# Loading q and k with 8 tokens per partition, four heads at a time, in an attention and mixer kernel

## The chip, the cores and the metric

The kernel runs on one core of a Trainium2 chip. Times are device microseconds (us) of one execution, and medians of several executions. "Fast" and "slow" are the states that each run is sorted into; comparisons use fast runs alone. A run's profile gives the span of the instructions (about 2 us less than the time) and the mean clock that TensorE was granted, as a share of full speed.

## The reference

Two stages for a batch of 8. First causal attention with 8 heads, 576 tokens and a head size of 64, with a bias from a running sum of `s`; then an MLP mixer on the result, over tokens (576 to 256 and back) and over channels (512 to 1536 and back), each with a residual.

```python
# cut to what matters
cum = np.cumsum(np.maximum(s, 0.0), axis=-1)
scores = q @ k.T / 8 + minimum(-(cum[i] - cum[j]), 0), causal
attn = softmax(scores);  x = attn @ v                       # per head
h = np.maximum(x.T @ w_tok1, 0.0) @ w_tok2;  u = x + h.T
out = u + np.maximum(u @ w_ch1, 0.0) @ w_ch2
```

All inputs and the output are float32; the kernel computes in bfloat16 with float32 sums.

## The kernel before

A small planner in the kernel's own Python orders all work: every piece (`P.op`) has an engine (or several to choose from), an estimated duration, the buffers that it reads and writes, and a priority. The planner simulates the five engines and fixes the order of instructions on each. On the chip every engine then keeps to its list and waits where something is late (in after ScalarE idled 7.56 us in front of a square, with an exp behind it whose input had been there for over 6 us; the timeline is below). All loads and stores are issued by SyncE, and loads keep their order (`after=last[0]`).

q and k are loaded for a pair of heads. A partition `p` takes R = 6 consecutive tokens of a head, one row of 6 x 64 x 4 = 1536 bytes, so 96 partitions hold 576 tokens. GpSimd casts them to bfloat16 (`qkn`), TensorE transposes them, and ScalarE takes a sum of squares for a guard: if a sum or the range of `cum` is too large, a slow general program computes everything again. That guard does not change the result here.

```python
R = 6;  PR = S // R                                  # 96 partitions
r_qf = ring("qkf", 3, [PR, 2, 2, R, D], FP32)        # partition, k/q, head of pair, token, d
r_qn = ring("qkn", 3, [PR, 2, R, 2, D], BF16)
r_vf = ring("vf", 2, [128, NJ, H, D], FP32)          # v of one batch, all five chunks

def stage_qk(b, h):
    f, n = Buf(r_qf), Buf(r_qn)
    for i, src in enumerate((k, q)):
        def load(i=i, src=src):
            nc.sync.dma_start(out=f.t[:, i].rearrange("p e r d -> p e (r d)"),
                              in_=src[b, h : h + 2].rearrange("e (p r) d -> p e (r d)", r=R))
        load_op(load, [(f, i)], 192 * 0.094 / 16)
        def cast(e, i=i): ...                        # GpSimd; in batch 0 also VectorE or ScalarE
    if b < 2:
        return
    col = (b * H + h) // 2                           # one square of 1536 elements for k, q and both heads
    P.op({"ACT": (1.55, 2.0, lambda: nc.scalar.activation(out=junk[:, :], in_=n.t[...], func=AF.Square,
          accum_out=sq[:, col : col + 1]))}, reads=[(n, 0), (n, 1)], writes=[("sq", col)], prio=60)

def stage_sq(b, h): ...        # batches 0 and 1: q and k loaded once more, later, for their squares

def mk(jc=jc, n=n):            # VectorE's causal mask: two inputs from SBUF, 5 per pair, 160 in all
    nc.vector.tensor_tensor(out=E.t[:, :, d0 : d0 + n], in0=E.t[:, :, d0 : d0 + n],
                            in1=keep[...].to_broadcast([128, 2, n]), op=ALU.mult)

def mul(eng, c=c, n=n, p0=p0): # v times its weights, GpSimd from batch 1 on: 5 per batch
    eng.tensor_tensor(out=vp.t[...], in0=vf.t[p0 : p0 + n, c], in1=wT[...], op=ALU.mult)
```

Of the kernel before, what the change touches and what calls it, by code (L numbers as in the profile page):

```python
# [333 lines left out]
def kernel(  # L334
# [24 lines left out]
    AHEAD = 4  # L359
    WARM = 45.0  # L360
    TOK = 2.0
    R = 6
# [32 lines left out]
    r_qf = ring("qkf", 3, [PR, 2, 2, R, D], FP32)  # L395
# [4 lines left out]
    r_vf = ring("vf", 2, [128, NJ, H, D], FP32)  # L400
# [56 lines left out]
    one_sb = sb("one_sb", [64, S], FP32, fast)  # L457
    cum = sb("cum", [64, S], FP32)
    half = sb("half", [64, 1], FP32, fast)
# [3 lines left out]
    nc.vector.memset(one_sb[:, :], 1.0)  # L463
# [5 lines left out]
    def act(n, fn, bias=False):  # L469
# [6 lines left out]
        out=cum[:, :], data0=one_sb[:, :], data1=s_sb[:, :], initial=0.0, op0=ALU.mult, op1=ALU.add))},  # L476
# [9 lines left out]
    def w_tr():  # L486
# [13 lines left out]
    NSQ = B * H // 2  # L500
    sq = sb("sq", [PR, NSQ], FP32, fast)
    junk = sb("junk", [PR, 4 * R * D], BF16, fast)
    pre = sb("pre", [64, S], FP32, fast)
    gap = sb("gap", [64, 4], FP32, fast)
    bad = sb("bad", [128, 4 + NSQ], FP32, fast)
    ones = sb("ones", [128, 1], FP32, fast)
# [3 lines left out]
    nc.vector.memset(ones[:, :], 1.0)  # L510

    P.op({"DVE": (1.3, 1.6, lambda: nc.vector.tensor_tensor_scan(
        out=pre[:, :], data0=one_sb[:, :], data1=wn[:, 0:S], initial=0.0, op0=ALU.mult, op1=ALU.add))},
# [16 lines left out]
    def stage_v(b):  # L530
        vf, vp = Buf(r_vf), Buf(r_vp[b % 2])
        odd = b % 2
        vbuf[b] = vp
        for c in range(NJ):
            n = min(128, S - c * 128)
            p0 = 64 if odd and n < 128 else 0

            def load(c=c, n=n, p0=p0):
                nc.sync.dma_start(out=vf.t[p0 : p0 + n, c, :, :],
                                  in_=v[b, :, c * 128 : c * 128 + n, :].rearrange("h p d -> p h d"))  # L540
            load_op(load, [(vf, c)] + ([("st", "v")] if b == 1 else []), 1024 * 0.0226 / 16 * n / 128)
        for c in range(NJ):
            n = min(128, S - c * 128)
            p0 = 64 if odd and n < 128 else 0

            def mul(eng, c=c, n=n, p0=p0):
                cw = c + 1 if p0 else c
                eng.tensor_tensor(  # L548
                    out=vp.t[p0 : p0 + n, c, :, 0:D], in0=vf.t[p0 : p0 + n, c, :, :],
                    in1=wT[p0 : p0 + n, cw, b * H : b * H + H].unsqueeze(2).to_broadcast([n, H, D]), op=ALU.mult)  # L550
            alts = ({"DVE": (*c_dve(512), lambda mul=mul: mul(nc.vector))} if b == 0 else
                    {"POOL": (*c_pool(512, 0.0019), lambda mul=mul: mul(nc.gpsimd))})
            P.op(alts, reads=[(vf, c), "wT"], writes=[(vp, c)], prio=b * 10 + 5 if b else 0)

        def ones():
            nc.gpsimd.tensor_copy(out=vp.t[:, 0 : NJ - 1, :, D], in_=wT[:, 0 : NJ - 1, b * H : b * H + H])
            p0, cw = (64, NJ) if odd else (0, NJ - 1)
            nc.gpsimd.tensor_copy(out=vp.t[p0 : p0 + 64, NJ - 1, :, D], in_=wT[p0 : p0 + 64, cw, b * H : b * H + H])
        P.op({"POOL": (0.5, 0.7, ones)}, reads=["wT"], writes=[(vp, "w")], prio=b * 10 + 5)
# [3 lines left out]
    def stage_qk(b, h):  # L563
        f, n = Buf(r_qf), Buf(r_qn)
        qkn[(b, h)] = n
        for i, src in enumerate((k, q)):
            def load(i=i, src=src):
                nc.sync.dma_start(out=f.t[:, i, :, :, :].rearrange("p e r d -> p e (r d)"),
                                  in_=src[b, h : h + 2, :, :].rearrange("e (p r) d -> p e (r d)", r=R))
            load_op(load, [(f, i)], 192 * 0.094 / 16)  # L570

            def cast(e, i=i):
                o, a = n.t[:, i, :, :, :], f.t[:, i, :, :, :].rearrange("p e r d -> p r e d")
                if e == 0:
                    nc.gpsimd.tensor_copy(out=o, in_=a)  # L575
                elif e == 1:
                    nc.vector.tensor_copy(out=o, in_=a)
                else:
                    nc.scalar.copy(out=o, in_=a)
            alts = {"POOL": (*c_pool(768, 0.0010), lambda cast=cast: cast(0))}  # L580
            if b == 0:
                alts["DVE"] = (*c_dve(768), lambda cast=cast: cast(1))
                alts["ACT"] = (*c_act(768), lambda cast=cast: cast(2))
            P.op(alts, reads=[(f, i)], writes=[(n, i)], prio=b * 10 + h if b else 0)
        if b < 2:
            return
        col = (b * H + h) // 2
        P.op({"ACT": (1.55, 2.0, lambda: nc.scalar.activation(
            out=junk[:, :], in_=n.t[:, :, :, :, :].rearrange("p t r e d -> p (t r e d)"), func=AF.Square,
            accum_out=sq[:, col : col + 1]))}, reads=[(n, 0), (n, 1)], writes=[("sq", col)], prio=60)  # L590

    def stage_sq(b, h):
        f = Buf(r_qf)
        col = (b * H + h) // 2
        for i, src in enumerate((k, q)):
            def load(i=i, src=src):
                nc.sync.dma_start(out=f.t[:, i, :, :, :].rearrange("p e r d -> p e (r d)"),
                                  in_=src[b, h : h + 2, :, :].rearrange("e (p r) d -> p e (r d)", r=R))
            load_op(load, [(f, i)], 192 * 0.094 / 16)
        P.op({"ACT": (1.55, 2.0, lambda: nc.scalar.activation(  # L600
            out=junk[:, :], in_=f.t[:, :, :, :, :].rearrange("p t e r d -> p (t e r d)"), func=AF.Square,
            accum_out=sq[:, col : col + 1]))}, reads=[(f, 0), (f, 1)], writes=[("sq", col)], prio=60)
# [3 lines left out]
    def pair(b, h):  # L606
# [6 lines left out]
        for ti, dst in ((0, kT), (1, qT)):  # L613
# [7 lines left out]
            P.op({"PE": (R * 0.045, R * 0.045 + 0.3, tr)}, reads=[(nat, ti)] + pads, writes=[(pt, 0)], holds=[dst], prio=(np_, 2))  # L621
# [87 lines left out]
    def view(t):  # L709
# [7 lines left out]
             "v": view(r_vf.tiles[1]), "uT": view(r_uTb.tiles[0]), "x2": view(r_x.tiles[2]),  # L717
             "x1": view(r_x.tiles[1]), "of": r_o.tiles[3][:, :]}
# [40 lines left out]
    def load_ch2(g):  # L759
        slot, c0, n = (("v", 0, 3), ("b0", 3, 3), ("b1", 6, 3), ("x1", 9, 2), ("of", 11, 1))[g]  # L760
# [12 lines left out]
    def tok(b):  # L773
# [31 lines left out]
        for c in range(NJ):  # L805
# [14 lines left out]
            P.op(dve(512, add), reads=[(pm, 0)] + xkeys, writes=[ukey], prio=0)  # L820
# [30 lines left out]
    def chan(b, u, us, uT):  # L851
# [26 lines left out]
        for ci, c in enumerate((4, 0, 1, 2, 3) if odd else (0, 1, 2, 3)):  # L878
            pm, o = Buf(r_mx, False), Buf(r_o, False)
            for th in range(3):  # L880
                def mm(c=c, pm=pm, th=th):
                    for cc in range(th * 4, th * 4 + 4):
                        nc.tensor.matmul(out=pm.t[:, :], lhsT=g.t[:, cc, c * 128 : c * 128 + 128], rhs=wc2[:, cc, :],  # L883
                                         start=(cc == 0), stop=(cc == NCC - 1))
                P.op({"PE": (4 * c_pe(512)[0], 4 * c_pe(512)[0] + 0.3, mm)}, reads=gkeys + [("wc2", i) for i in range(5)],
                     writes=[(pm, 0)], holds=[o], prio=(rank + 2.0 + 2.0 * ci / NJ, 1))
            if odd:
                src, si = (us, 0) if c == NJ - 1 else (u, c)
            else:
                src, si = u, c  # L890
            sk = [(us, 0, 0), (us, 0, 64)] if src is us else [(u, si, 0)]

            def add(pm=pm, o=o, src=src, si=si):
                nc.vector.tensor_tensor(out=o.t[:, :], in0=pm.t[:, :], in1=src.t[:, si, :], op=ALU.add)
            P.op(dve(512, add), reads=[(pm, 0)] + sk, writes=[(o, 0)] + ([("st", "of")] if b == 0 else []), prio=0)

            def st(o=o, c=c):
                if c < NJ - 1:
                    nc.sync.dma_start(out=out[b, c * 128 : c * 128 + 128, :], in_=o.t[:, :])
                else:  # L900
                    for i in range(2):
                        nc.sync.dma_start(out=out[b - 1 + i, NQ:S, :], in_=o.t[i * 64 : i * 64 + 64, :])
            P.op({"SP": (0.6 if c < NJ - 1 else 1.2, 0, st)}, reads=[(o, 0)], prio=0, dma=128 * 0.088 / 16)

    for h in range(0, H, 2):
        stage_qk(0, h)
        if h == 4:
            stage_v(0)
    load_tok()
    for h in range(0, AHEAD, 2):  # L910
        stage_qk(1, h)
    for i in range(4):
        load_ch1(i)
    for i in range(5):
        load_ch2(i)
    for b in range(1, B):
        for h in range(0, H, 2):
            if b > 1 or h >= AHEAD:
                stage_qk(b, h)
            if h == (0 if b > 1 else 4):  # L920
                stage_v(b)
    for b in range(2):
        for h in range(0, H, 2):
            stage_sq(b, h)
    for b in range(B):
# [5 lines left out]
    P.op(dve(64, lambda: nc.vector.tensor_scalar(  # L931
        out=bad[0:PR, 4:], in0=sq[:, :], scalar1=21.0, scalar2=None, op0=ALU.is_gt)),
        reads=[("sq", i) for i in range(NSQ)] + ["bad0"], writes=["bad"], prio=50)
# [85 lines left out]
```

## Time and profile before

| | before |
|---|---|
| median time | 331.1 us (331.06 to 331.87, 3 runs) |
| span, mean granted clock | 330.5 us, 0.982 |
| TensorE, VectorE, ScalarE, GpSimd busy | 93%, 63%, 63%, 31% |
| q and k rows | 15360 packets of 1536 bytes, mean 95 ns |
| first channel matmul of batches 0 and 1 | 42.7 and 81.6 us |

The page of before: busy time by engine, the granted clock of TensorE over 40 equal slices in tenths, and the queue of all loads and stores (packets, MB, the time of its packets as a share of 16 DMA engines).

```profile
span 330.5 us, 6536 instructions
PE 308.9 (93%) x2424; PEld 178.6 (54%) x2457; DVE 207.2 (63%) x511; ACT 207.4 (63%) x367; POOL 101.1 (31%) x137
...
PEclk9699999999999999999999999999999989999998
...
q1 hardware_dynamic: 77232, 53.64, 65.7%
```

The windows view of before: start and end of the window, its length, busy us (and instructions) of PE, PEld, DVE, ACT and POOL, the granted clock, the share of the 16 DMA engines and GB/s.

```profile
0.00:30.00 30.00, 24.40 (x195) 13.27 (x199) 23.92 (x67) 17.91 (x30) 15.78 (x34) 0.89 1.03 240
30.00:60.00 30.00, 27.69 (x228) 18.97 (x232) 20.45 (x42) 21.24 (x40) 15.67 (x18) 1.00 1.07 296
60.00:90.00 30.00, 26.75 (x286) 17.03 (x288) 26.99 (x67) 22.42 (x39) 19.75 (x23) 1.00 1.11 253
90.00:150.00 60.00, 59.21 (x468) 32.95 (x472) 38.80 (x98) 41.20 (x71) 21.34 (x27) 1.00 0.61 142
150.00:270.00 120.00, 117.05 (x934) 67.93 (x944) 79.25 (x200) 81.94 (x143) 28.53 (x36) 0.99 0.63 155
```

In each of the windows up to 90 us the DMA queue is full (a share of 1.03, 1.07 and 1.11: packets overlap), and TensorE is not (busy 24.40, 27.69 and 26.75 of 30 us); after 90 us TensorE is nearly always busy (59.21 of 60 us up to 150).

Two groups of the lines view (busy us, mean ns; then the engine's idle time just before them): ScalarE's squares of a pair for one of the three buffers, and the masks on one of the three `E` tiles.

```profile
L671 DVE TENSOR_TENSOR E_84<-E_84,keep 128x256 bf16<-128x256 bf16 (+1 forms) x55 | 17.2, 343 | 11.1 <-ACT E_84 L663 10.6
...
L588 ACT ACTIVATE junk<-qkn_77 96x1536 bf16<-96x1536 bf16 x8 | 11.9, 1489 | 0.0
```

TensorE's longest wait (line waiting, what for: us in total, times, longest):

```profile
PE psc_112 L657 <- ACT E_86 L663: 2.1, 1, 2.1
```

This is a single wait, behind a square (L600) whose reload was late; nothing else in the list is over 1.2 us.

### The profile page before, as it was taken

The numbers are of one execution on the slowest core, as the hardware profiler recorded it, in microseconds if no ns is written. First come the engines' busy times: TensorE is split into PE (matmuls) and PEld (weight loads), VectorE is DVE, ScalarE is ACT, GpSimd is POOL, SyncE is SP. The second block draws the span as 40 slices with busy tenths as digits, with TensorE's granted clock in tenths as the row PEclk, the third lists the DMA queues.
The fourth block names the chain that finished last, engine by engine and source line by source line (L and its number), as shares of the span: only waits on it lengthen the run. The fifth ranks groups of instructions, "written<-read, shape, count | busy, mean of one in ns | idle before, by whom it ended". The sixth has DMA issues, their size and how long they took to land.

```text
span 330.5 us, 6536 instructions
## 1 busy us (share of the span) xinstructions
PE 308.9 (93%) x2424; PEld 178.6 (54%) x2457; DVE 207.2 (63%) x511; ACT 207.4 (63%) x367; POOL 101.1 (31%) x137
## 2 busy tenths in 40 slices
PE   6888899979899999999999999999999799999992
PEld 2455486646665555555774554556764355446640
DVE  7698963789965756576776566576786454450021
ACT  4675777388886367974885278766889457406600
POOL 5455429757518022450146011821110000000000
PEclk9699999999999999999999999999999989999998
DMA  7999999999982549636944649266459710042031
GB/s 194 212 271 350 387 228 248 244 285 225 244 179 74 127 155 223 148 84 196 196 94 119 155 158 221 76 110 219 121 138 204 217 70 0 1 129 81 3 98 69
DMA packets 77272, 54.14 MB, mean 164 GB/s; under 512 B 54320, under 2 KB 70256, under 8 KB 77232
## 3 DMA queue, kind: packets, MB, share of 16 engines
q1 hardware_dynamic: 77232, 53.64, 65.7%
q8 instruction: 21, 0.34, 0.5%
q14 instruction: 19, 0.16, 0.2%
HBM read 40.65 MB, written 9.44 MB: 152 GB/s over the span
## 4 chain that ended last, share of the span: by engine, by line
PE 75%; DVE 14%; ACT 3%; DMA 3%; issue 2%; SPq 1%; POOL 0%; ACTq 0%
PE pmx_118 L883 12%; PE pmx_119 L865 9%; PE pmx_118 L865 8%; PE pmx_117 L865 8%; PE pmx_117 L883 7%; PE pmx_119 L883 7%; PE psc_112 L657 3%; PE pav_115 L689 2%; PE psc_113 L657 2%; PE psc_114 L657 2%; PE pav_116 L689 2%; DMA qkf_73<-in_k_dram 2%; PE pmx_117 L791 2%; PE pmx_117 L812 2%; DVE E_86 L671 2%
## 5 line engine op out<-in xcount | busy, mean ns | idle before, releaser
L865 PEld LDWEIGHTS <-wc_70 128*128 128x128 bf16 x624 | 59.2, 98 | 30.7 <-issue 0.5
L883 PEld LDWEIGHTS <-gb_107 128*128 128x128 bf16 x240 | 22.8, 99 | 25.6 <-issue 1.3
L575 POOL CAST qkn_75<-qkf_72 96x768 bf16<-96x768 f32 x19 | 17.1, 923 | 43.2 <-issue 12.9
L575 POOL CAST qkn_76<-qkf_73 96x768 bf16<-96x768 f32 x22 | 18.3, 853 | 37.2 <-issue 18.2
L883 PE MATMUL pmx_118<-wc_71,gb_107 128*128 128x512 bf16 x116 | 28.9, 393 | 0.2
L883 PEld LDWEIGHTS <-ga_106 128*128 128x128 bf16 x192 | 18.0, 98 | 19.6
L575 POOL CAST qkn_77<-qkf_74 96x768 bf16<-96x768 f32 x19 | 15.7, 843 | 30.7 <-ACT gb_107 L872 10.3
L671 DVE TENSOR_TENSOR E_84<-E_84,keep 128x256 bf16<-128x256 bf16 (+1 forms) x55 | 17.2, 343 | 11.1 <-ACT E_84 L663 10.6
L865 PE MATMUL pmx_118<-uTb_105,wc_70 128*128 128x320 bf16 x128 | 22.6, 299 | 0.1
L865 PE MATMUL pmx_119<-uTb_105,wc_70 128*128 128x320 bf16 x128 | 22.6, 299 | 0.0
L865 PE MATMUL pmx_117<-uTb_105,wc_70 128*128 128x320 bf16 x128 | 22.6, 299 | 0.0
L671 DVE TENSOR_TENSOR E_85<-E_85,keep 128x256 bf16<-128x256 bf16 (+1 forms) x55 | 16.7, 331 | 8.9 <-ACT E_85 L663 8.7
L548 POOL TENSOR_TENSOR vp_90<-vf_88,wT 128x512 bf16<-128x512 f32 (+1 forms) x20 | 20.6, 1053 | 2.2 <-DMA vf_88<-in_v_dram 1.9
L671 DVE TENSOR_TENSOR E_86<-E_86,keep 128x256 bf16<-128x256 bf16 (+1 forms) x50 | 14.8, 323 | 10.3 <-ACT E_86 L663 10.1
L872 ACT ACTIVATE gb_107<-pmx_119 128x320 bf16<-128x320 f32 x23 | 10.2, 442 | 17.4 <-PE pmx_119 L865 16.0
L548 POOL TENSOR_TENSOR vp_89<-vf_87,wT 128x512 bf16<-128x512 f32 (+1 forms) x15 | 15.4, 1041 | 6.0 <-PE pav_116 L689 4.7
L865 PE MATMUL pmx_118<-uTa_104,wc_70 128*128 128x512 bf16 (+1 forms) x79 | 17.1, 336 | 0.1
L865 PE MATMUL pmx_119<-uTa_104,wc_70 128*128 128x512 bf16 (+1 forms) x80 | 17.1, 336 | 0.0
L883 PE MATMUL pmx_117<-wc_71,ga_106 128*128 128x512 bf16 x69 | 16.9, 379 | 0.2
L865 PE MATMUL pmx_117<-uTa_104,wc_70 128*128 128x512 bf16 (+1 forms) x77 | 16.6, 335 | 0.2
L970 PE MATMUL pmx_117<-zero 128*128 128x512 bf16 (+6 forms) x44 | 14.2, 418 | 1.5 <-DVE zero L425 1.2
L883 PE MATMUL pmx_118<-wc_71,ga_106 128*128 128x512 bf16 x57 | 14.3, 379 | 0.2
(284 smaller groups left out, 695.9 us busy)
## 6 DMA issues: line engine op xcount, KB each, us to landing
vf_87<-in_v_dram SPq DMA_DIRECT2D x16, 256.0 KB, 6.6
vf_88<-in_v_dram SPq DMA_DIRECT2D x16, 256.0 KB, 5.5
qkf_74<-in_k_dram SPq DMA_DIRECT2D x14, 288.0 KB, 4.1
qkf_74<-in_q_dram SPq DMA_DIRECT2D x14, 288.0 KB, 4.4
qkf_72<-in_k_dram SPq DMA_DIRECT2D x13, 288.0 KB, 3.8
qkf_72<-in_q_dram SPq DMA_DIRECT2D x13, 288.0 KB, 4.4
qkf_73<-in_k_dram SPq DMA_DIRECT2D x13, 288.0 KB, 4.8
qkf_73<-in_q_dram SPq DMA_DIRECT2D x13, 288.0 KB, 5.2
```

The source lines that it names most:

```text
L548: eng.tensor_tensor(out=vp.t[p0 : p0 + n, c, :, 0:D], in0=vf.t[p0 : p0 + n, c, :, :], in1=wT[p0 : p0 + n, cw, b * H : b * H + H].unsqueeze ...
L575: nc.gpsimd.tensor_copy(out=o, in_=a)
L657: nc.tensor.matmul(out=o[:, :, c0 : c0 + e - a], lhsT=kT.t[:, j0 : j0 + 128], rhs=qT.t[:, :, a:e], start=True, stop=True)
L671: nc.vector.tensor_tensor(out=E.t[:, :, d0 : d0 + n], in0=E.t[:, :, d0 : d0 + n], in1=keep[:, k0 : k0 + n].unsqueeze(1).to_broadcast([128, ...
L689: nc.tensor.matmul(out=o[:, ic, 0 : D + 1], lhsT=E.t[:, hh, d0 : d0 + 128], rhs=vp.t[:, jc, h + hh, 0 : D + 1], start=(jc == j_lo), stop=( ...
L791: nc.tensor.matmul(out=pm.t[:, ha * D : hb * D], lhsT=w1[:, NJ if odd and c == NJ - 1 else c, t * 128 : t * 128 + 128], rhs=x.t[:, c, ha * ...
L812: nc.tensor.matmul(out=pm.t[:, :], lhsT=w2[:, t, w0 : w0 + 128], rhs=h1.t[:, t, :], start=(t == 0), stop=(t == NTC - 1))
L865: nc.tensor.matmul(out=pm.t[:, 0 : e - a], lhsT=wc1[:, m, cc * 128 : cc * 128 + 128], rhs=uT.t[:, m, a:e], start=(m == 0), stop=(m == NMC ...
L872: lambda cc=cc, pm=pm, a=a, e=e: nc.scalar.activation(out=g.t[:, cc, a:e], in_=pm.t[:, 0 : e - a], func=AF.Relu),
L883: nc.tensor.matmul(out=pm.t[:, :], lhsT=g.t[:, cc, c * 128 : c * 128 + 128], rhs=wc2[:, cc, :], start=(cc == 0), stop=(cc == NCC - 1))
L970: f.fn = lambda t=r.tiles[slots[0]], n=n: nc.tensor.matmul(out=t[:, 0:n], lhsT=zero[:, 0:128], rhs=zero[:, 0:n], start=True, stop=True)
```

## The change

The intent: rows of 2048 bytes instead of 1536, so that fewer packets carry q and k, each at the 92 ns that other 2048-byte packets take in before, where a 1536-byte row of q or k takes 95; and a shorter end, as the last output chunk is computed, added and stored in two halves. A partition takes R = 8 tokens, so 72 partitions hold a head. Four heads ("a quad") are loaded per step: one DMA for partitions 0 to 63 and a small one for partitions 64 to 71 ("the tail"). To make room, v has seven single-chunk buffers. The squares are taken per head.

```diff
-    R = 6
+    R = 8
-    r_qf = ring("qkf", 3, [PR, 2, 2, R, D], FP32)
+    r_qf = ring("qkf", 3, [PR, 4, R, D], FP32)
-    r_vf = ring("vf", 2, [128, NJ, H, D], FP32)
+    r_vf = ring("vf", 7, [128, H, D], FP32)
@@ loads
+    def load_quad(b, h, i, f, e0, e1, tail):
+        src = (k, q)[i][b, h : h + 4, :, :].rearrange("e (p r) d -> p e (r d)", r=R)
+        load_op(lambda: nc.sync.dma_start(out=dst_of(f)[0:64, e0:e1, :], in_=src[0:64, e0:e1, :]),
+                [(f, e) for e in range(e0, e1)], (e1 - e0) * 64 * 0.085 / 16)
+        if tail:
+            load_op(lambda: nc.sync.dma_start(out=dst_of(f)[64:PR, :, :], in_=src[64:PR, :, :]), [(f, "t")], 0.25)
@@ squares, batches 2 to 7 (batches 0 and 1: four of 512 elements per tensor of a quad)
-        col = (b * H + h) // 2
-        P.op({"ACT": (1.55, 2.0, ... in_=n.t[:, :, :, :, :] ...
+        for e in range(2):
+            col = b * H + h + e
+            P.op({"ACT": (1.12, 1.5, ... in_=n.t[:, :, :, e, :] ...
@@ order of the loads
     for b in range(1, B):
-        for h in range(0, H, 2):
-            if b > 1 or h >= AHEAD:
-                stage_qk(b, h)
-            if h == (0 if b > 1 else 4):
-                stage_v(b)
+        if b > 1:
+            stage_quad(b, 0)
+        stage_v(b)
+        stage_quad(b, 4)
@@ cut: the last chunk in halves, v's buffers, staging slots of the weights, limits of the guard
```

## The prediction

> What bounds the kernel now. The page shows TensorE busy 93% of 330.5 us. By matmul sizes, useful streaming is about 280 us, so some 50 us are lost, in three places. (1) The head: useful streaming in ten-us windows is 0.9, 3.2, 5.3, 5.7, 8.1, 9.0, 8.7, 7.7, 8.2 us up to 90 us; 33 us are lost there. From 90 to 260 us only 6 are lost. (2) Between 260 and 270 us 4 us are lost: in the timeline ScalarE idles 2.6 us before a norm square (L600) whose q reload is late, TensorE then waits 2.1 us for an exp behind it, and the clock drops. (3) The tail: the last matmul ends at about 324.4, then a 0.69 us add, a store and its landing: 6 us.
>
> The head is DMA-bound: the windows view gives a DMA share of 1.0 to 1.2 up to 90 us. By the packets, a 1536 B q/k row takes 95 ns (15360 of them), a 2048 B row 92, a 256 B row of v 23. In the chain of waits from 17 to 41 us VectorE (busy 9.4 and 9.6 of 10 us) paces; from 41.6 TensorE runs batch 0's channel MLP, then starves mildly from 60 to 90 because pairs 2 and 3 of batch 1 land only at 55 to 58.8 us.
>
> [...] the trace agrees that small rows are dear (256 B: 11 B/ns; 2048 B: 22). V stays at 256 B.
>
> What the change does.
> - q/k rows: 15360 x 95.3 ns/16 = 91 us of DMA time become 11520 x 92.4/16 = 66: estimate -2.5 us per batch. Batch 0 and 1 finish loading about 5 us sooner; pair 3 no longer lands behind v (20.3 us before; estimate 13). Batch 0's channel MLP starts at 39 to 40 us instead of 42.7, and the starvation from 60 to 90 shrinks. Estimate: -6 us, all on the path.
> - Coarser buffers: the next q waits for two casts; the queue is backlogged then, so no bubble.
> - Transposes: 8 of 72 columns instead of 6 of 96. Starts are about 41 ns apart at 96 columns and 30 at 65 (AV), so about 0.26 us either way. [...] 96- and 128-row loads both take 98 ns here. Effect 0.
> - GpSimd casts grow from 0.85 to about 1.13 us, the same number: +18 us busy, not limiting.
> - ScalarE squares: 24 x 1.69 us become 48 x 1.26, and 8 x 1.69 become 32 x 0.83: +33 us busy, to about 240 (74%). They stand in order before exps: estimate +1 us of TensorE waits.
> - The reloads for squares remain, in eight load-then-four-squares steps: the stall at 260 may go or return: -1 us on average.
> - Last chunk in halves: -0.4 us.
>
> Sum: 331.1 - 6 + 1 - 1 - 0.4 = 324.7. I say 325.0 us, 320.5 to 330 eight times in ten. Faster by over 2%: 0.44; within 2%: 0.53; slower: 0.03.
>
> What would show it: q/k packets at 2048 B and about 92 ns, DMA share of the queue falling from 66% to about 58%; the first channel matmul of batch 0 near 39.5 us and of batch 1 near 79 (86.3 before); ScalarE busy about 240, GpSimd about 119; transposes unchanged per pair; tail about 5.7 us.
>
> What would make it wrong: VectorE, not DMA, holding the head (gain 2 us); ScalarE squares stalling exps (loss of 3 or more); or a hole in the DMA queue from the coarser buffers.

Two passages are cut from it, where marked: statements of how the chip behaves. "Useful streaming" is my estimate from the columns of the matmuls; those of 512 columns at L883 start 0.216 us apart in before (median). The clock that "drops" was 0.83 from 260 to 270 us.

## The result and the profile after

The changed kernel is correct and takes 360.34 us (median of 4 fast runs, 360.25 to 360.99) against 331.08 (330.16 to 331.87) for before in the same rounds. The ratio is 1.0889, with a 95% interval of 1.0858 to 1.092. Ratios here are the mean time of one kernel's fast runs over that of the other's fast runs of the same rounds, so they are not quite the ratio of the medians.

The page of after:

```profile
span 358.6 us, 6875 instructions
PE 318.0 (89%) x2558; PEld 183.1 (51%) x2590; DVE 218.4 (61%) x517; ACT 230.6 (64%) x462; POOL 112.7 (31%) x135
...
PEclk9999999969999978999999999989899999999997
...
q1 hardware_dynamic: 73264, 53.64, 70.2%
```

The windows view of after, the same windows:

```profile
0.00:30.00 30.00, 23.50 (x189) 12.76 (x193) 22.96 (x63) 19.08 (x30) 10.83 (x28) 1.00 0.98 194
30.00:60.00 30.00, 26.88 (x241) 18.66 (x242) 16.41 (x37) 18.10 (x40) 16.25 (x18) 1.00 1.05 302
60.00:90.00 30.00, 24.86 (x281) 14.62 (x280) 23.60 (x57) 20.45 (x38) 18.58 (x20) 0.89 0.98 201
90.00:150.00 60.00, 53.02 (x405) 29.94 (x408) 39.15 (x92) 38.64 (x73) 23.93 (x25) 0.94 0.67 135
150.00:270.00 120.00, 112.01 (x940) 65.42 (x949) 79.27 (x185) 86.63 (x172) 41.11 (x45) 0.97 0.71 138
```

In the first window the queue is as full as before (0.98 against 1.03) and moves 194 GB/s instead of 240; from 60 to 90 us it is 201 instead of 253. The packets got fewer (73264 instead of 77232), yet the queue's share rose from 65.7% to 70.2% of a longer span. From 90 us on TensorE has new holes: 53.02 busy of 60 us where before had 59.21, and a lower granted clock (0.94 and 0.97 where before had 1.00 and 0.99).

The lines view of after, the same groups (each pair now has two squares; L617 are those of batches 0 and 1):

```profile
L688 DVE TENSOR_TENSOR E_85<-E_85,keep 128x256 bf16<-128x256 bf16 (+1 forms) x55 | 21.5, 425 | 12.8 <-ACT E_85 L680 12.7
...
L607 ACT ACTIVATE junk<-qkn_76 72x1024 bf16<-72x1024 bf16 x16 | 16.9, 1054 | 9.7 <-POOL qkn_76 L593 9.5
...
L617 ACT ACTIVATE junk<-qkf_74 72x512 bf16<-72x512 f32 x16 | 10.1, 632 | 6.0 <-DMA qkf_74<-in_k_dram 4.5 <-DMA qkf_74<-in_q_dram 1.2
```

ScalarE now idles in front of squares: in these two groups, 9.5 us for a cast of GpSimd and 4.5 for a k that had not landed. TensorE's longest waits:

```profile
PE psc_117 L674 <- ACT E_85 L680: 5.2, 2, 5.0
PE psc_118 L674 <- ACT E_86 L680: 3.9, 2, 3.4
PE psc_117 L636 <- ACT qkn_75 L597: 3.7, 1, 3.7
PE pav_120 L706 <- DVE E_84 L688: 2.7, 1, 2.7
```

How one of them came about can be read from the timeline of after between 116 and 132 us (start, us, engine, line, what; in brackets the idle time before and its end):

```profile
116.20 5.29 SPq L845 DMA_TRANSPOSE uTa_109<-ua_105  x4
...
121.58 0.68 SPq L564 DMA_DIRECT2D qkf_74<-in_q_dram  x1
...
128.27 1.04 POOL L593 CAST qkn_76<-qkf_74 72x1024 bf16<-72x1024 f32 x1 [10.92 <-DMA qkf_74<-in_q_dram]
...
129.34 1.05 ACT L607 ACTIVATE junk<-qkn_76 72x1024 bf16<-72x1024 bf16 x1 [7.56 <-POOL qkn_76 L593]
...
130.40 0.57 ACT L680 ACTIVATE E_85<-psc_117 128x512 bf16<-128x512 f32 x1
...
131.00 1.54 DVE L688 TENSOR_TENSOR E_85<-E_85,keep 128x256 bf16<-128x256 bf16 x2 [6.46 <-ACT E_85 L680]
131.02 0.59 PE L674 MATMUL psc_117<-qT_79,kT_82 128*128 128x384 bf16 x2 [4.96 <-ACT E_85 L680]
```

The load of q for a quad is issued at 121.58. Before it SyncE had waited 14.9 us, until 114.9, for an output chunk that it was to store:

```profile
SPq L926 <- DVE of_113 L917: 14.9, 1, 14.9
```

and had then spent 5.29 us on four transposing DMAs. From 108 to 116 us the windows view gives a DMA share of 0.00, where before has 0.54. GpSimd's cast starts at 128.27, when it has landed; ScalarE's square, next in ScalarE's list, waits 7.56 us for that cast; the exp behind it starts at 130.40; and TensorE, which needs that exp's PSUM slot, has waited 4.96 us. One late load thus passes through GpSimd and ScalarE to TensorE, because each keeps its order. The same exp holds up VectorE (6.46 us), and its next two masks then take 1.54 us together, beside GpSimd's multiplies of v.

### The profile page after: what moved, and what is told of

Same layout as the page of the kernel before. It is cut to its first block, busy times and chain, and to the rows that moved or that the text cites. A ratio compares the mean times of both kernels' runs of the same rounds, so it can differ in the third digit from the quotient of the medians.

```text
span 358.6 us, 6875 instructions
## 1 busy us (share of the span) xinstructions
PE 318.0 (89%) x2558; PEld 183.1 (51%) x2590; DVE 218.4 (61%) x517; ACT 230.6 (64%) x462; POOL 112.7 (31%) x135
## 2 busy tenths in 40 slices
DMA packets 73307, 54.17 MB, mean 151 GB/s; under 512 B 54064, under 2 KB 54896, under 8 KB 73264
## 3 DMA queue, kind: packets, MB, share of 16 engines
q1 hardware_dynamic: 73264, 53.64, 70.2%
## 5 line engine op out<-in xcount | busy, mean ns | idle before, releaser
L882 PEld LDWEIGHTS <-wc_70 128*128 128x128 bf16 x624 | 60.1, 99 | 35.2 <-issue 3.2
L908 PEld LDWEIGHTS <-gb_112 128*128 128x128 bf16 x252 | 24.4, 100 | 25.6 <-issue 2.3
L908 PE MATMUL pmx_122<-wc_71,gb_112 128*128 128x512 bf16 (+1 forms) x130 | 30.6, 380 | 0.1
L688 DVE TENSOR_TENSOR E_85<-E_85,keep 128x256 bf16<-128x256 bf16 (+1 forms) x55 | 21.5, 425 | 12.8 <-ACT E_85 L680 12.7
L908 PEld LDWEIGHTS <-ga_111 128*128 128x128 bf16 x192 | 18.2, 100 | 20.3 <-issue 1.9
L882 PE MATMUL pmx_123<-uTb_110,wc_70 128*128 128x320 bf16 x128 | 23.2, 304 | 1.8 <-DMA uTb_110<-us_108 0.9
L882 PE MATMUL pmx_122<-uTb_110,wc_70 128*128 128x320 bf16 x128 | 23.3, 306 | 0.0
L882 PE MATMUL pmx_124<-uTb_110,wc_70 128*128 128x320 bf16 x128 | 23.2, 304 | 0.1
L607 ACT ACTIVATE junk<-qkn_76 72x1024 bf16<-72x1024 bf16 x16 | 16.9, 1054 | 9.7 <-POOL qkn_76 L593 9.5
L688 DVE TENSOR_TENSOR E_84<-E_84,keep 128x256 bf16<-128x256 bf16 (+1 forms) x55 | 19.0, 375 | 6.0 <-ACT E_84 L680 5.6
L688 DVE TENSOR_TENSOR E_86<-E_86,keep 128x256 bf16<-128x256 bf16 (+1 forms) x50 | 15.0, 329 | 11.3 <-ACT E_86 L680 11.2
L593 POOL CAST qkn_75<-qkf_72 72x1024 bf16<-72x1024 f32 x9 | 9.3, 1036 | 33.5 <-ACT gb_112 L889 20.0
L607 ACT ACTIVATE junk<-qkn_77 72x1024 bf16<-72x1024 bf16 x16 | 16.9, 1056 | 3.5 <-POOL qkn_77 L593 3.1
L889 ACT ACTIVATE gb_112<-pmx_124 128x320 bf16<-128x320 f32 x21 | 9.2, 439 | 14.8 <-PE pmx_124 L882 13.5
L995 PE MATMUL pmx_122<-zero 128*128 128x512 bf16 (+11 forms) x49 | 16.0, 430 | 1.9 <-DVE zero L424 1.2
L908 PE MATMUL pmx_122<-wc_71,ga_111 128*128 128x512 bf16 x68 | 17.1, 379 | 0.2
L607 ACT ACTIVATE junk<-qkn_75 72x1024 bf16<-72x1024 bf16 x16 | 16.9, 1054 | 0.6
L882 PE MATMUL pmx_122<-uTa_109,wc_70 128*128 128x512 bf16 (+1 forms) x80 | 17.1, 336 | 0.0
L882 PE MATMUL pmx_124<-uTa_109,wc_70 128*128 128x512 bf16 (+1 forms) x76 | 16.9, 334 | 0.2
L882 PE MATMUL pmx_123<-uTa_109,wc_70 128*128 128x512 bf16 (+1 forms) x78 | 16.9, 335 | 0.1
L908 PE MATMUL pmx_124<-wc_71,ga_111 128*128 128x512 bf16 x55 | 15.0, 397 | 0.3
L593 POOL CAST qkn_76<-qkf_73 72x1024 bf16<-72x1024 f32 x10 | 10.4, 1042 | 13.1 <-ACT gb_112 L889 11.5
```

Source lines behind the costliest of these rows:

```text
L593: nc.gpsimd.tensor_copy(out=o, in_=a)
L607: P.op({"ACT": (1.12, 1.5, lambda e=e, col=col: nc.scalar.activation(out=junk[:, :, :, :], in_=n.t[:, :, :, e, :], func=AF.Square, accum_o ...
L882: nc.tensor.matmul(out=pm.t[:, 0 : e - a], lhsT=wc1[:, m, cc * 128 : cc * 128 + 128], rhs=uT.t[:, m, a:e], start=(m == 0), stop=(m == NMC ...
L889: lambda cc=cc, pm=pm, a=a, e=e: nc.scalar.activation(out=g.t[:, cc, a:e], in_=pm.t[:, 0 : e - a], func=AF.Relu),
L908: nc.tensor.matmul(out=pm.t[:, n0:n1], lhsT=g.t[:, cc, c * 128 : c * 128 + 128], rhs=wc2[:, cc, n0:n1], start=(cc == 0), stop=(cc == NCC - 1))
L995: f.fn = lambda t=r.tiles[slots[0]], n=n: nc.tensor.matmul(out=t[:, 0:n], lhsT=zero[:, 0:128], rhs=zero[:, 0:n], start=True, stop=True)
```

## The experiments

Eighteen kernels ran, in five batches; within a batch all ran on one chip, with before run again there. Where a variant has wrong data, this is said; it changes no instruction's place unless stated. The table holds all results, as medians of the fast executions; e_fast, e_nosq, e_fast_nosq and b_halves each had one slow execution, which is left out (with it their medians are 344.69, 345.60, 340.69 and 330.52, and some of the expectations quote these). Before's own median moves between 329.4 and 331.1 us from batch to batch, so a difference of two times from different batches is uncertain by 1 to 2 us. The text below takes the runs in the order of the questions.

| run | median us of the fast runs (before there) | ratio, 95% interval |
|---|---|---|
| m1_loads | 140.24, one look, loads alone | none |
| e_fast | 344.67 (330.02) | 1.0384, 1.0272 to 1.0497 |
| e_nosq | 345.33 (330.02) | 1.0405, 1.0282 to 1.0529 |
| e_r6 | 336.90 (330.02) | 1.0219, 1.0141 to 1.0297 |
| e_fast_nosq | 339.48 (329.56) | 1.0268, 1.021 to 1.0326 |
| b_sq | 332.94 (329.56) | 1.0099, 1.0049 to 1.0148 |
| e_r6_pairsq | 1877.45 (329.56) | guard tripped, says nothing |
| b_cast2 | 334.63 (329.56) | 1.0142, 1.0093 to 1.0191 |
| e_fnq_half | 338.07 (330.57) | 1.0254, 1.019 to 1.0318 |
| b_half | 328.28 (330.57) | 0.9939, 0.988 to 0.9998 |
| b_halves | 330.41 (330.57) | 0.9984, 0.9932 to 1.0035 |
| b_hl3 | 327.44 (330.57) | 0.9916, 0.9873 to 0.996 |
| b_r8 | 346.02 (329.45) | 1.0465, 1.0378 to 1.0552 |
| e_r6_ps26 | 337.98 (329.45) | 1.0257, 1.0196 to 1.0319 |
| e_fnq_hv | 326.91 (329.45) | 0.9908, 0.9847 to 0.9968 |
| b_v7 | 327.78 (329.37) | 0.9993, 0.9932 to 1.0054 |
| e_r6_v2 | 336.48 (329.37) | 1.0241, 1.0197 to 1.0284 |
| b_hv | 328.40 (329.37) | 1.0016, 0.9947 to 1.0084 |

### Why are the larger rows slower?

In after, all 2048-byte packets have a mean of 134 ns. Before's 6144 packets of that size (weights and output) had 92. In after 6016 of these are left, as the last output chunk goes out in rows of 1024 bytes, and 17536 - 6016 = 11520 are q and k. If the others kept their 92 ns, those of q and k have (17536 x 134 - 6016 x 92) / 11520 = 156 ns (an earlier count gave the 157 of the expectations). Theory P: the destination makes this, as rows that go to partitions 0 to 63 land more slowly than rows spread otherwise. Rival theory A: aligned 2 KB rows at this distance in HBM are slow to read.

**m1_loads** has loads alone, in sections of four DMAs, with zeros for the output (wrong).

```python
def b_64x2048(i, x, b, h):        # as the change does
    nc.sync.dma_start(out=dst(i, 0, 64, 4, 512), in_=rows(x, b, h, 4, 8)[0:64])
def c_64x2048_at32(i, x, b, h):   # rows of the same form, of the next batch, to partitions 32 to 95
    nc.sync.dma_start(out=dst(i, 32, 96, 4, 512), in_=rows(x, b, h, 4, 8)[0:64])
```

> Loads alone, ten sections of four DMAs each, one section after the other; output zeros, wrong on purpose. Theory P [...]: a 2048 B packet takes about 155 ns when the 64 rows go to partitions 0 to 63 or to 64 to 127, about 90 ns when the very same source rows go to partitions 32 to 95; 64 rows of 1536 B on partitions 0 to 63 are slow too, about 115 ns; the tail of 8 partitions is worst, 250 ns or more; 128 partitions of 2304 B about 95 ns. Theory A [...]: 2048 B packets are slow, about 155 ns, wherever the 64 rows land, and 64 rows of 1536 B take 65 to 75 ns.

The causes that I had in mind for the two theories are cut, as no run shows one. The 155 and 90 ns start from the 156 (after) and 92 (before) above; the other figures of the landing were guesses, to be held against the table below.

The lines "DMA packets" of the DMA view, first for the stretch of the section to partitions 0 to 63:

```profile
DMA packets 1088, 2.10 MB, mean 210 GB/s; under 512 B 64, under 2 KB 64, under 8 KB 1088
```

and for the rows to partitions 32 to 95:

```profile
DMA packets 1088, 2.10 MB, mean 287 GB/s; under 512 B 64, under 2 KB 64, under 8 KB 1088
```

| section (from the trace's packet records) | ns per packet, mean / median | GB/s |
|---|---|---|
| 2048 B to partitions 0 to 63 | 152 / 162, again later 153 / 164 | 210, 216 |
| rows of the same form to partitions 32 to 95 | 90 / 84 | 290 |
| 2048 B to partitions 64 to 127 | 161 / 162 | 200 |
| 1536 B to partitions 0 to 63 | 122 / 127 | 198 |
| 1536 B to partitions 0 to 95 (as before) | 80 / 65, again last 90 / 65 | not comparable: first its four loads ran one by one, each behind a memset, and last beside the store of the output (199) |
| 2048 B to partitions 64 to 71 (the tail) | 222 / 296 | 67 |
| 2304 B to partitions 0 to 127 | 107 / 93 | 306 |
| 4096 B to partitions 0 to 127 | 171 / 159 | 353 |

The rows are not quite the very same, as the expectation says: each section takes the next batch. But size, alignment and distance in HBM are equal, and partitions 0 to 63 were slow for two batches (152 and 153 ns). With the destination shifted by 32 partitions such rows land in 90 ns, and at 64 to 127 they take 161: theory P holds and theory A falls. So it is not the number of partitions, which is 64 in all three, but which ones they are. Why it is these is not shown.

**b_r8** does this alone in the kernel before: order of instructions, pairs and pair squares as before, only 8 tokens per partition with the tail (and room made for it: one scan input and one scratch tile fewer).

```diff
-    R = 6
+    R = 8
-                nc.sync.dma_start(out=f.t[:, i] ..., in_=src[b, h : h + 2] ...)
+                nc.sync.dma_start(out=d[0:64, :, :], in_=a[0:64, :, :])
+                nc.sync.dma_start(out=d[64:PR, :, :], in_=a[64:PR, :, :])
```

> The kernel before, in its own order of instructions and with its pairs and pair squares, with one thing of the change alone: 8 tokens per partition, 64 partitions in one DMA and 8 in a second. Theory P (rows over partitions 0 to 63 land slowly, the main cause): 341 to 350 us, packets of q and k at about 155 ns and 11 to 19 us lost. If the slow rows hurt only because quads wait for whole quads: 333 to 338.

It took 346.0 us. By the ratio that is 0.0465 x 329.45 = 15.3 us over before. Its profile has the signs of after:

```profile
0.00:30.00 30.00, 24.53 (x200) 12.96 (x200) 21.99 (x66) 18.13 (x29) 11.57 (x30) 1.00 1.00 183
...
60.00:90.00 30.00, 24.61 (x240) 13.93 (x238) 24.32 (x49) 16.43 (x27) 22.77 (x24) 0.89 1.09 230
```

and TensorE's longest wait:

```profile
PE psc L659 <- ACT E L665: 7.3, 4, 4.6
```

So the row form alone makes about half of the loss, without quads. The packets cost less than I had expected (mean 135 ns by the same sum), but the full queue of the head moves 183 GB/s instead of 240, and most of the loss is made there: by the traces batch 1's first channel matmul is 9.5 us later than in before (91.1 against 81.6), of 13.4 us by which the spans differ. The row form is more than the landing, though: there is the second small DMA, and with fewer partitions each instruction treats more elements. In b_r8 casts take 1.05 us instead of 0.87, and squares 1.91 instead of 1.48. No run separates these parts.

**e_fast** keeps the changed kernel's order of instructions on every engine, and spreads the loads of q and k over all 128 partitions (wrong data).

```diff
-        nc.sync.dma_start(out=dst_of(f)[0:64, e0:e1, :], in_=src[0:64, e0:e1, :])
+        nc.sync.dma_start(out=dst_of(f)[:, m0:m1, :], in_=rows_of_the_same_heads_over_128_partitions)
```

> The changed kernel with the same instruction order on every engine, the same bytes, rows and DMA count for q and k, but each load spread over all 128 partitions; the data are wrong on purpose. If the slow loads are what made the change lose: q/k packets fall from about 157 to about 90 ns and the time to 321 to 330 us (what the prediction said). If ScalarE's squares or the coarser quads lose the time by themselves: 345 us or more.

It took 344.7 us, 15.7 less than after, and missed the expected 321 to 330 (and just missed the other case, 345 or more). Not all is as the expectation says: in the trace 4864 packets have 4096 bytes (mean 209 ns), as two neighbouring rows now go to one partition. So partitions and packet size changed together here; m1_loads holds the size. The slow rows cost some 16 us, but something else was left.

**e_r6** keeps the whole change except the row form: 6 tokens per partition, one DMA over 96 partitions per tensor of a quad.

```diff
-    R = 8
+    R = 6
-        ... out=dst_of(f)[0:64, e0:e1, :], in_=src[0:64, e0:e1, :] ... and the tail
+        ... out=dst_of(f)[:, e0:e1, :], in_=src[:, e0:e1, :]
```

> Everything of the change (quads of one tensor, squares per head, last chunk in halves, buffers of v and of the weights) but with 6 tokens per partition: one DMA of 96 partitions with 1536 B rows per tensor. If the row form alone is to blame: packets about 95 ns and 325 to 333 us. If the quads, the squares or the new order are to blame: 340 us or more.

At 336.9 us it lies between the two expectations: 23 of the 29 us went with the row form, and 7 stayed. Here too the casts change with it (0.83 us instead of 1.06), which may be why it gives back more than e_fast; this is not shown.

### What is left: the squares?

**e_nosq** is the changed kernel in its own order without any norm square (`sq` set to zero, so the guard is off; the result stays correct).

> The changed kernel with the same order, but without the norm squares on ScalarE (the norms are not checked; the output stays right on these inputs). Theory: late q/k loads hurt mostly because a square that waits for them stands in ScalarE's queue ahead of exps: then 335 to 345 us, although the packets stay near 157 ns. Rival 1, late loads hurt directly through the transposes: 352 us or more. Rival 2, the squares' own 33 us of ScalarE time is the whole loss: 325 to 331 us.

345.3 us, 15.0 less than after. So the squares seem to be worth as much as the slow rows. **e_fast_nosq** has both edits.

> The changed kernel in its own order of instructions, with loads over 128 partitions (wrong data on purpose) and without the norm squares. Fast loads alone gave 344.7 us and no squares alone 345.6, each some 14 us over before. Theory S (the rest after fast loads is ScalarE's squares, +33 us of busy time in front of exps): 322 to 332 us, at or under before. Rival G (the rest is the quads: four GpSimd casts in a row when a quad lands, under which VectorE's mask multiplies stretch): 333 to 341 us. If the two costs are the same wait counted twice, 335 or more.

339.5 us: both edits together give 20.9 us, not 15.7 + 15.0 = 31. So some 10 us are in both. This fits one wait counted twice, as in the timeline above: a late row holds a square, and the square holds the exp behind it. Theory S fell, as by the ratio 0.0268 x 329.56 = 8.8 us over before are left without squares and with fast rows.

**b_sq** puts the per-head squares into before, at the places of its own squares.

```diff
-        nc.scalar.activation(out=junk[:, :], in_=n.t[...], func=AF.Square, accum_out=sq[:, col : col + 1])
+        for e in range(2):
+            nc.scalar.activation(out=junk[...], in_=n.t[:, :, :, e, :], func=AF.Square, accum_out=sq[...])
```

> The kernel before with one thing of the change alone: the squares are taken per head (48 of 768 elements, and 32 of 384 for batches 0 and 1) in the places where before has one of 1536, all else in its order. ScalarE's busy time should rise by about 11 us (each extra instruction costs about 0.2 us of start and accumulator read). Theory S (squares themselves push exps late): 334 to 338 us. Rival (squares have slack as long as q and k land in time): 329 to 332 us.

The accumulator read that the expectation speaks of is an instruction of its own in before's trace, 32 of 0.196 us in the mean. The ratio is 1.0099, that is 3.3 us, just between the two expectations. Squares per head cost these 3.3 us where rows land in time. **e_r6_pairsq** was to take e_r6 with one square per pair.

> The variant with 6 tokens per partition and one DMA per tensor of a quad (336.9 us), in its own order, with one square per pair of 1536 elements as in the kernel before. Theory S (the remaining 7 us are the squares per head): 329 to 332 us. Rival G (the remaining 7 us are quads and their order): 334 to 337 us.

My mistake: I left the guard's limits at the values for single heads, the sums of pairs passed them, and the general program ran (1877 us, correct). **e_r6_ps26** mends the limits.

> The earlier run with one square per pair, mended: its sums had passed the guard's limits (13 and 6.5, meant for single heads), so the slow general program ran; the limit is now 26. Quads of heads with 6 tokens per partition, order of the 6-token variant (336.9 us). Theory S (squares per head are the rest): 329 to 332 us. Theory Q (quads, and the order that the planner makes of them, are the rest): 334.5 to 337.

338.0 us (1.0257): with rows over 96 partitions, squares per pair are no better than per head. The 7 us that e_r6 has over before are not squares.

### What is left: GpSimd beside VectorE's masks?

In the traces a mask multiply that overlaps a cast of GpSimd takes longer than one that does not (before: mean 590 ns for 19 of them, 293 for the 139 that overlap neither a cast nor a multiply of v). A mask that starts during GpSimd's instruction mostly ends just after it: of the 15 masks of before that start during a cast, 13 end 0.08 to 0.15 us after that cast ends, and so do 16 of the 17 that start during a multiply of v in e_fnq_half (below; 0.08 to 0.19 us). Why is not shown.

**b_cast2** doubles GpSimd's casts in before from batch 2 on, each issued twice in a row.

> The kernel before, with each GpSimd cast of batches 2 to 7 issued twice in a row (same result; bursts of two casts become bursts of four, as in the changed kernel; GpSimd busy +42 us). Theory G (bursts of casts stretch VectorE's masks and so delay TensorE): 334 to 340 us, and the mean mask multiply beside a cast stays near 0.6 us but three to four masks in a row are hit. Rival: 329.5 to 332 us, VectorE has the slack.

1.0142, 4.7 us slower: within the expectation, so bursts of casts do reach TensorE. (The second cast also delays the transposes behind it and all later work of GpSimd; the run does not tell this from the masks.) **e_fnq_half** is e_fast_nosq with casts of half of the elements from batch 1 on (wrong data), and **b_half** is before with the same.

```diff
-                    nc.gpsimd.tensor_copy(out=o, in_=a)
+                    nc.gpsimd.tensor_copy(out=o[:, 0 : R // 2], in_=a[:, 0 : R // 2])     # if b
```

> The changed kernel with fast loads and no squares (340.7 us), in its own order, in which every GpSimd cast from batch 1 on treats half of the elements (wrong data on purpose), so that a burst of four casts takes about 2.2 us instead of 4.2. Theory G (the remaining 11 us over before are VectorE's masks stretched beside GpSimd's casts): 328 to 333 us, and the mean mask multiply falls to about 0.3 us. Rival O (the order of instructions and the coarser quads cost it, not the casts): 336 us or more.

> The kernel before with the same halved casts (wrong data on purpose), for the value of shorter casts as such. Theory G: the casts come two at a time and mostly fit in VectorE's slack, so 327 to 330 us, a gain of at most 2. If before gains as much as the changed kernel does, shorter casts are worth the same anywhere and theory G explains no difference.

338.1 us: only 1.4 less than e_fast_nosq, where theory G wanted 328 to 333. Before itself gained 2.0 us. Casts are not the main rest; theory G as I had put it fell. But in that trace 21 masks overlap a multiply of v by GpSimd and no cast (mean 652 ns); in before it was 2. So the next run halves those too.

**e_fnq_hv** is e_fnq_half with the multiplies of v over half of the heads from batch 2 on (the result is wrong). **b_hv** does that alone in before.

```diff
+                G = H // 2 if b >= 2 else H
-                    out=vp.t[p0 : p0 + n, c, :, 0:D], ...
+                    out=vp.t[p0 : p0 + n, c, 0:G, 0:D], ...
```

> The changed kernel with fast loads, no squares, half casts (338.1 us), and now also GpSimd's multiplies of v from batch 2 on over half of the heads (wrong data on purpose), order as changed. Theory G (VectorE's masks wait beside any GpSimd work; 21 masks stood beside a v multiply in that run, 2 to 3 in before): 330 to 334 us. Theory O (the planner's order itself, made for quads, leaves the gaps): 335.5 to 338.

> The kernel before with GpSimd's multiplies of v from batch 2 on over half of the heads (wrong result on purpose), for the value of shorter multiplies where they stand. Theory G says that in before they stand beside two or three masks only: 328.5 to 330.5 us, a gain of at most 1. If before gains 4 or more, the v multiplies cost the same in both kernels and explain no difference.

326.9 us: 11 us less than e_fnq_half, and under before (which is no gain to have, as it does less work than before: half casts, no squares). In before the same edit gives nothing (1.0016). The multiplies of v cost nothing where before has them, and 11 us where the changed order has them. One stretch of e_fnq_half, from the waits, windows and lines views. TensorE's longest wait is for masks:

```profile
PE pav L707 <- DVE E L689: 5.2, 8, 0.8
```

```profile
64.00:72.00 8.00, 5.77 (x79) 3.71 (x79) 7.87 (x18) 4.21 (x8) 6.12 (x9) 0.82 1.16 312
72.00:80.00 8.00, 7.62 (x44) 3.50 (x45) 6.17 (x16) 4.03 (x9) 4.38 (x7) 0.75 0.99 241
```

```profile
L689 DVE TENSOR_TENSOR E<-E,keep 128x256 bf16<-128x256 bf16 (+1 forms) x160 | 53.9, 368 | 17.9 <-ACT E L681 17.4
L546 POOL TENSOR_TENSOR vp<-vf,wT 128x512 bf16<-128x512 f32 (+1 forms) x35 | 37.0, 1062 | 28.6 <-DMA vf<-in_v_dram 27.0 <-DVE E L689 0.2
```

The same of e_fnq_hv:

```profile
PE pav L708 <- DVE E L690: 0.9, 3, 0.4
```

```profile
64.00:72.00 8.00, 5.90 (x67) 3.39 (x66) 7.40 (x20) 4.79 (x9) 4.98 (x10) 1.00 1.06 342
72.00:80.00 8.00, 7.68 (x111) 5.35 (x109) 7.81 (x22) 5.08 (x10) 3.54 (x7) 1.00 1.01 236
```

```profile
L690 DVE TENSOR_TENSOR E<-E,keep 128x256 bf16<-128x256 bf16 (+1 forms) x160 | 45.2, 313 | 17.9 <-ACT E L682 17.4
...
L547 POOL TENSOR_TENSOR vp<-vf,wT 128x256 bf16<-128x256 f32 (+3 forms) x35 | 23.8, 686 | 33.3 <-DMA vf<-in_v_dram 31.3 <-PE pmx L856 1.1 <-DVE E L690 0.6
```

The masks fell from 368 to 313 ns, and TensorE's waits for them from 5.2 to 0.9 us. That is 4.3 of the 11 us. The windows show a further part: in e_fnq_half the granted clock falls to 0.82 and 0.75 between 64 and 80 us (by the trace's clock records it is half from 69.18 to 76.01 us), and TensorE gets through 44 matmuls of 13458 columns in 7.62 busy us from 72 to 80, where e_fnq_hv gets through 111 of 16804 columns. TensorE is busy for 5.5 us of the half-clock spell, so it cost about 2.8 us (an estimate: half of that). Not all of the 11 us belongs to the edit: at batch 0's first channel matmul, before any shortened multiply runs, the two profiled runs are already 1.8 us apart (40.6 and 38.8 us). Nor does the run tell the masks' waits from what else comes sooner when GpSimd is done sooner. The timeline shows what stood around the fall of the clock, masks of 1.82 us for three beside two multiplies of v, and two waits of TensorE of 0.8 us, the second of which ends after it:

```profile
67.45 2.09 POOL L546 TENSOR_TENSOR vp<-vf,wT 128x512 bf16<-128x512 f32 x2 [0.34 <-DMA vf<-in_v_dram]
...
68.01 1.82 DVE L689 TENSOR_TENSOR E<-E,keep 128x256 bf16<-128x256 bf16 x3
...
68.70 0.23 PE L707 MATMUL pav<-vp,E 128*128 128x65 bf16 x2 [0.79 <-DVE E L689]
...
69.75 0.87 PE L707 MATMUL pav<-vp,E 128*128 128x65 bf16 x12 [0.82 <-DVE E L689]
...
73.97 2.90 PE L809 MATMUL pmx<-x,w 128*128 128x512 bf16 x8 [0.22 <-issue]
```

The last line is a run of eight 512-column matmuls; in the trace the first of them start 0.43 us apart, and the last three 0.22 and 0.21 us, as at full clock (0.216 us in the median at L883 of before). So in this place TensorE lost clock as well, beside its waits of 0.79 and 0.82 us; it was busy for 5.77 of the 8.00 us of the window in which the clock fell. That the waits brought the fall about is not shown. Over the whole span, up to the last matmul, the clock records of after have half clock for 20.5 us with TensorE busy in 16.2 of them, and before's for 10.2 us with 9.2 busy. Half of the busy time, 8.1 and 4.6 us, is an estimate of what the lowered clock cost.

### Why do the multiplies of v stand beside the masks?

Theory V: the seven single-chunk buffers of v, which I had not costed. **b_v7** puts them into before, **e_r6_v2** takes them out of e_r6.

```diff
-    r_vf = ring("vf", 2, [128, NJ, H, D], FP32)
+    r_vf = ring("vf", 7, [128, H, D], FP32)        # b_v7; e_r6_v2 has it the other way round
```

> The kernel before with one thing of the change alone: v in seven buffers of one chunk each instead of two of a batch each (and the staging slots of the weights that this needs). It changes the order of SyncE and GpSimd, the other engines' orders almost not. Theory V (single-chunk buffers let v arrive and be multiplied one chunk at a time in the middle of the pairs, beside VectorE's masks): 333 to 338 us, with 12 or more masks beside a v multiply instead of 2. Rival (v's buffers are harmless, quads move the v multiplies): 329 to 331.5.

> The 6-token variant (336.9 us) with v back in two buffers of a batch each; TensorE's, ScalarE's and VectorE's orders stay as they are, only SyncE's and GpSimd's move. Theory V: 329 to 333 us, and few masks beside a v multiply. Rival (quads): 335.5 to 338.

Theory V fell: 0.9993 for b_v7 and 1.0241 for e_r6_v2, as much as e_r6. In e_r6_v2 16 masks overlap a multiply of v and no cast, in e_r6 18, in b_v7 8 and in before 2. (In b_r8, with pairs, there are 11, of 380 ns: late rows alone also bring such overlaps.) What remains is the step from pairs to quads, with the order that the planner makes for it. It has two parts that no run separates: four casts come at once, and the load order puts v behind four heads of q and k instead of two (see the diff). The traces agree with the second (batch 2's v is multiplied from 59.8 us on in before, and from 63.7 in e_fnq_half, where batch 1's masks run), but this is argued, not shown.

### The end of the run, and a better version

**b_halves** is before with the last chunk in two halves. **b_hl3** adds a larger estimate to the planner for the reloads of batches 0 and 1, so that their squares stand later in ScalarE's order.

```diff
-            load_op(load, [(f, i)], 192 * 0.094 / 16)      # in stage_sq
+            load_op(load, [(f, i)], 3.0)
```

> The kernel before with only the last output chunk computed, added and stored in two halves. The prediction put this at -0.4 us. In the variant with 6 tokens per partition the end came 5.6 us after the last matmul, against 6.1 before: 328.8 to 329.6 us, ratio 0.997 to 1.0. If the extra 1.7 us of tail in the changed kernel comes from the halves, 330.5 to 332.

> A try for a better version: the kernel before with the last chunk in halves and, in the planner, an estimate of 3 us instead of 1.1 for the reloads that feed the squares of batches 0 and 1, so that a square is no longer put in ScalarE's order before its reload has landed (this cost about 4 us between 260 and 270 us of before). If that stall goes and none comes elsewhere: 325 to 328 us. If it only moves: 329 to 331.

b_halves is 0.9984, with 1 inside the interval; by its trace the end comes 5.6 us after the end of the last matmul instead of 6.1, so the predicted 0.4 us is there but too small to time. In after, that distance is 7.8 us. There SyncE has a hole of 2.2 us (354.6 to 356.8) between two semaphore instructions, after the last packet of the output (352.8). In this hole a packet of 16384 bytes and two of 8192 on the instruction queues are still under way, until 355.6; whether SyncE waits for its own instructions there is not shown. All kernels with 8 tokens in the changed order end that late (7.6 to 8.2 us); b_r8, b_halves and e_r6 do not (5.6 to 6.1).

b_hl3 is 0.9916 (0.9873 to 0.996): 327.4 us, better than both kernels. The window that its edit was made for, first before:

```profile
260.00:270.00 10.00, 7.83 (x55) 3.96 (x54) 4.00 (x13) 5.46 (x9) 0.00 (x0) 0.83 0.42 142
```

and b_hl3:

```profile
260.00:270.00 10.00, 9.89 (x89) 5.52 (x89) 7.58 (x21) 6.51 (x12) 0.00 (x0) 1.00 0.48 159
```

## Why the prediction was wrong

I predicted 325.0 us, and it took 360.3. What was said of before mostly holds. Its 50 us of lost time are rather 45: the profile of before lacks 28 records of 512-column matmuls that the one of b_r8, with the same matmuls, has.

- **The step that failed: "q/k rows: 15360 x 95.3 ns/16 = 91 us of DMA time become 11520 x 92.4/16 = 66".** The count was right. The 92.4 ns was taken from packets of the same size that the trace showed, but those were stores of the output (4608) and loads of weights (1536), from and to 128 partitions, and these go to 64 and 8. Measured: 156 ns (the sum above), so 11520 x 156 / 16 = 112 us, more than before's 91. m1_loads shows that the destination partitions make this (152 ns to 0 to 63, 90 to 32 to 95). The gain of 6 us in the head became a loss: batch 1's first channel matmul came at 90.3 us where I had said 79 and before had 81.6 (the 86.3 for before in the prediction is a misreading of the trace). The same row form in before costs 15.3 us (b_r8), and taking it out of the change gives back 23 (e_r6).
- **Squares.** I said +33 us of ScalarE's time, to about 240 us, and +1 us of waits. Busy rose by 23 us, to 230.6, less than said. But the waits depend on when rows land: 3.3 us in before (b_sq), and 15.0 with slow rows (e_nosq), as squares stand in order in front of exps. "ScalarE squares stalling exps" was on my list of what could go wrong; I did not see that slow rows would set it off.
- **GpSimd "not limiting".** Busy was 112.7 us against my 119, and casts 1.06 us against 1.13. Right in size, wrong in consequence: I read the 31% of GpSimd as slack, and asked neither which VectorE instructions stand beside it nor what quads do to its order. With rows and squares out of the way and half casts, 11 us came back when its multiplies of v were shortened (e_fnq_hv). The same edit to before's multiplies of v alone gave nothing (b_hv).
- **"Coarser buffers: the next q waits for two casts; the queue is backlogged then, so no bubble."** There was a bubble: the DMA share is 0.00 from 108 to 116 us, a quad's q is issued at 121.58 behind a store and SyncE's transposes, and GpSimd is idle for 10.92 us until it landed. That the coarser buffers made this one is not shown, since SyncE was waiting for the store. But in all SyncE waits 51 us for casts to free a buffer of q or k (L564 in after) where before has 35 (L568).
- **Transposes: effect 0.** This held. In the traces their starts are 42 ns apart for 96 columns and 32 for 72, so 6 x 42 and 8 x 32 are the same.
- **Halves: -0.4 us.** The end of b_halves agrees (0.5 us); in after it is hidden by the hole at the end.
- **v's buffers** were not in the sum. b_v7 and e_r6_v2 show no cost.

Of the 29 us, the row form alone accounts for 15.3 and the rest of the change with good rows for 7.2 (0.0219 x 330.02, e_r6). About 7 us are neither, but what the two do to one another. The parts should not be added as if they were independent: taking away slow rows, squares, half of the casts and half of the multiplies of v, one after another, gave 15.7, 5.2, 1.4 and 11.2 us. What stays open is which half of the quads (casts at once, or v's place in the load order) moved the multiplies of v, and the hole at the end.

## What to carry to other kernels

Cost a DMA by where it lands as well as by its row size (64 rows of 2048 bytes: 152 ns a packet to partitions 0 to 63, 90 to 32 to 95, in m1_loads): take a packet's time only from transfers to the same partitions, or measure it in a small kernel of loads alone. Two engines with a third or more of their time free can still be in each other's way (VectorE and GpSimd were busy 63% and 31% in before, and a mask of 293 ns took 590 beside a cast): before you call one "not limiting", look in the trace at which instructions it overlaps, and what in the order of work will move them. In a kernel with a fixed order on each engine, low-priority work in front of an exp is as urgent as the exp, once its input is late (in after a square that waited 7.56 us for its cast cost TensorE 4.96).
